# Two-pass 64-bit weight conversion with signs from GpSimd, and layer norm's Newton steps per group of tiles

## The chip, the cores and the metric

One core of a Trainium2 chip runs the whole program. The metric is device time in microseconds for one execution, with all inputs in device memory before and the output there after it.

## What is computed

Eight batches go through three blocks. The first is an attention with 32 memory slots per head; the second mixes the tokens by a low-rank product and applies a wide two-layer network (512 to 2048 to 512); the third is a gated network whose gate is layer-normalised and mixed over the tokens.

```python
a = softmax(phi, axis=seq)                 # 8 batches, 8 heads, 576 tokens, 32 slots
k_m, v_m = a.T @ k, a.T @ v
x = softmax(q @ k_m.T / 8) @ v_m           # heads joined: 8 x 576 x 512
u = x + (x.T @ U @ V).T
y = u + relu(u @ w_ch1) @ w_ch2            # 512 -> 2048 -> 512
h = relu(y @ w_in);  u, v = h[..., :512], h[..., 512:]
v_n = (v - mean(v)) / sqrt(var(v) + 1e-6)
out = (u * (w_spatial @ v_n + b_spatial)) @ w_out
```

U, V, w_ch1, w_ch2, w_in and w_out arrive as 64-bit floats (they are products of 32-bit arrays and 64-bit scalars), so the kernel turns them into 32-bit floats on the chip. The other inputs are 32-bit.

## The kernel before

Tokens stand in tiles of 128 (four, and one of 64), the 512 features in four blocks of 128. From batch 1 on, each matmul runs as three products of 16-bit high and low parts; batch 0 runs its large matmuls in 32 bits, while the weights are still being loaded, converted and split.

**Conversion.** `conv_stream` (L868) works through 22 chunks of 128 x 1024 weights: per quarter c of w_ch1 two chunks of w_ch1 and two of w_ch2, then four of w_in and two of w_out (chunks 20 and 21). A chunk is 1 MB of 64-bit words and lands in one of seven buffers, which `seq` names: two in the later z tile, two in the w_in tile, one each in those of w_out, of the spatial weights and of y (yraw). `load` (L894) lets a chunk be loaded only when the chunk that had its buffer has been converted. The loads, like all other DMAs, are issued from SP in order.

A raw chunk is read as pairs of 32-bit words, low and high. `conv_a` (L166): ScalarE (ACT) takes the absolute value of the high word into the destination, scaled so that a shift by three gives the 32-bit exponent (L167); VectorE (DVE) moves the top three bits of the low word down by 13 within 16-bit halves (L169) and keeps the sign bit of the high word beside them (L170). `conv_b` (L172): DVE shifts the destination left by three and joins it with these bits (L174). Then `square` (L911) squares the converted chunk on ACT (L182 for w_ch1, L184 for the others, in `conv_square`); for w_ch1 PE sums the squares over partitions (L918) and DVE takes their maximum (L920). After the last chunk of a weight `scale_w` (L238) finds its scale through DVE, PE (L125), DVE (L127, L144) and GpSimd (POOL; L110 and L108 are the lines of the helper `ps2`). GpSimd has no other part in the conversion.

**Order.** The program is traced in a fixed order, and a scheduler places each instruction on its engine; an engine then works strictly in that order. The `Filler` (L830) mixes the conversion into batch 0's matmuls: a call `fl(4.0, cs)` in `batch0` (L1071) advances the conversion's generator until the costs it yields (0.7 after conv_a, 1.2 after conv_b) use up the budget. `need(n)` advances it until n chunks are converted. `behind(i)` (L905) puts the DVE instructions of chunks 3 and up behind the first attention's last DVE pass (`marks[2]`, a subtraction at L404); chunks 0 to 2 may be placed among the first attention's passes. The first attention (`att(0)`, L302) also converts U and V (`setup_small`, L199) with the same two functions.

Batch 0's first half of tokens runs in four quarters c: `z_first` (L525, eviction L537), `w1_first` (L539, matmuls L547, evictions L549), then `w2_start` and `w2_add` (L565, L570). The second half follows, during which the spatial weights are loaded (L1106), the remaining weights are split (L136 to L141) and batch 1's attention runs.

**Layer norm.** `v_tile` (L677) multiplies a token tile with half of w_in (L701), evicts it through Relu (L705), takes mean and variance on DVE (L707, L709), and finds 1/sqrt(var + 1e-6) by a shift, a subtraction and three Newton steps on one column (L721 to L731), each of which is two passes of `ps2` (L110). Then the mean is subtracted (L732). The last tile's 64 tokens stand as two halves of 256 features on 128 partitions, whose statistics are joined first (L710 to L720). `v_norm` (L735) scales the tile into its 16-bit parts on ACT and DVE (L739, L745 for the last tile). `V_ORDER` (L22) fixes how v_tile (v), v_norm (n) and u_half (u, L756) follow each other: v0 first, then the string. `spatial` (L779) needs all five tiles, the last one at L795.

## Time and profile before

| | us |
|---|---|
| three runs | 1213.47, 1216.18, 1216.71 (median 1216.18) |
| the profiled execution | 1213.53 |
| its span, first to last instruction | 1211.7 |
| PE matmuls busy | 1154.9 (95%) |
| DVE busy | 751.8 (62%) |
| ACT busy | 534.4 (44%) |
| POOL busy | 66.0 (5%) |

Batch 0 takes roughly the first 260 us, each later batch 138. The engines' names in the profile are PE (TensorE), DVE (VectorE), ACT (ScalarE), POOL (GpSimd) and SP (the DMA queue). Busy shares are means over the span, in which the stages have different limits. Times in a row count from the span's start.

### The profile page before, as it was taken

What the parts mean: (1) busy time and instruction counts of PE and PEld (TensorE: products, weight loads), DVE (VectorE), ACT (ScalarE), POOL (GpSimd) and SP (SyncE); (2) the same over time, 40 slices, a digit from 0 to 9 for tenths busy, and PEclk for the clock granted to TensorE, in tenths of its full rate; (3) what the DMA queues carried; (4) which work ended last, traced back from release to release, by engine and by line L of the source; (5) the groups of instructions that cost most, each with busy time, mean ns of one, the idle gap of its engine ahead of it and who ended that gap; (6) DMA issues with size and microseconds to landing.
All of it is one profiled execution on the core that took longest, in us unless ns stands there. A gap on an engine that the chain in (4) does not pass through costs nothing.

```text
span 1211.7 us, 24362 instructions
## 1 busy us (share of the span) xinstructions
PE 1154.9 (95%) x9988; PEld 861.4 (71%) x9991; DVE 751.8 (62%) x2107; ACT 534.4 (44%) x1213; POOL 66.0 (5%) x245
## 2 busy tenths in 40 slices
PE   5767999999999999999999999999999999999998
PEld 4534676667767787677768786677767787677766
DVE  5998567856756474755657465654658455642464
ACT  2655885565534342451434433442334424342333
POOL 1003000000000000000000000000000000000000
PEclk8789999999999999999999999999999999999999
DMA  9566330014000310014000220014000210010001
GB/s 331 209 236 233 129 100 21 1 41 138 22 1 21 119 40 21 1 40 139 21 1 14 92 74 21 1 40 130 26 6 1 75 31 2 1 40 2 1 1 40
DMA packets 45680, 74.61 MB, mean 62 GB/s; under 512 B 7232, under 2 KB 36544, under 8 KB 42624
## 3 DMA queue, kind: packets, MB, share of 16 engines
q1 hardware_dynamic: 45568, 73.05, 18.4%
q8 instruction: 78, 1.28, 0.5%
q14 instruction: 34, 0.28, 0.1%
HBM read 63.60 MB, written 9.44 MB: 60 GB/s over the span
## 4 chain that ended last, share of the span: by engine, by line
PE 81%; DVE 11%; DMA 4%; ACT 2%; POOL 1%; issue 1%; SPq 0%; DVEq 0%; ACTq 0%; POOLq 0%
PE mm L630 25%; PE mm L593 14%; PE mm L816 8%; PE mm L756 7%; PE mm L793 7%; PE mm L701 6%; PE mm L570 3%; PE at L380 2%; DMA kvt<-in_kv_dram 2%; PE at L518 1%; PE at L328 1%; PE at L417 1%; PE mm L547 1%; PE mm L698 1%; DMA yraw<-in_u_dram 1%
## 5 line engine op out<-in xcount | busy, mean ns | idle before, releaser
L630 PE MATMUL mm<-g,w2r 128*128 128x288 f16 x2688 | 347.5, 286 | 0.0
L630 PEld LDWEIGHTS <-w2r 128*128 128x128 f16 x2688 | 256.9, 98 | 76.0 <-issue 14.2
L593 PE MATMUL mm<-apr,z 128*128 128x288 f16 x1344 | 167.5, 286 | 0.0
L593 PEld LDWEIGHTS <-z 128*128 128x128 f16 x1344 | 131.2, 98 | 32.9
L648 ACT ACTIVATE y<-mm 128x288 f32<-128x288 f32 x56 | 22.7, 406 | 208.7 <-DVE tiny L131 208.7
L602 DVE TENSOR_TENSOR g<-tmp,g 128x288 f16<-128x288 f32 x224 | 99.2, 456 | 20.0 <-ACT g L599 16.7
L131 DVE TENSOR_REDUCE tiny<-mm 128x1 f32<-128x288 f32 x64 | 28.8, 453 | 126.4 <-PE mm L630 124.0
L793 PE MATMUL mm<-wsr,vu 128*128 128x288 f16 x768 | 104.7, 286 | 0.0
L597 ACT ACTIVATE tmp<-mm 128x288 f32<-128x288 f32 x224 | 91.8, 422 | 28.6 <-PE mm L593 14.5
L816 PE MATMUL mm<-ghl,wor 128*128 128x288 f16 x768 | 96.9, 286 | 1.2 <-ACT wor L140 1.2
L756 PE MATMUL mm<-yhl,wir 128*128 128x288 f16 x768 | 96.8, 286 | 0.0
L816 PEld LDWEIGHTS <-wor 128*128 128x128 f16 x768 | 74.7, 98 | 22.1 <-ACT wor L140 1.5
L756 PEld LDWEIGHTS <-wir 128*128 128x128 f16 x768 | 74.5, 98 | 21.6 <-issue 1.6
L793 PEld LDWEIGHTS <-vu 128*128 128x128 f16 x768 | 74.5, 98 | 18.5
L701 PE MATMUL mm<-wir,yhl 128*128 128x512 f16 x384 | 86.0, 379 | 0.0
L803 ACT ACTIVATE ghl<-vu,ysc 128x288 f16<-128x288 f32 x64 | 34.2, 534 | 81.5 <-DVE vu L802 60.1
L701 PEld LDWEIGHTS <-yhl 128*128 128x128 f16 x384 | 37.2, 98 | 41.7 <-issue 0.3
L570 PE MATMUL mm<-g,w2r 128*128 128x288 f32 x256 | 66.6, 413 | 0.2 <-issue 0.2
L570 PEld LDWEIGHTS mm<-g,w2r 128*128 128x128 f32 x256 | 48.3, 193 | 17.1 <-issue 2.7
L110 DVE TENSOR_SCALAR tiny<-tiny 128x1 f32<-128x1 f32 x240 | 57.1, 240 | 4.1
L601 DVE CAST g<-tmp 128x288 f16<-128x288 f32 x112 | 34.4, 307 | 40.4 <-ACT tmp L597 39.8
L599 ACT ACTIVATE g<-mm 128x288 f16<-128x288 f32 x112 | 46.7, 417 | 0.0
(231 smaller groups left out, 1548.5 us busy)
## 6 DMA issues: line engine op xcount, KB each, us to landing
kvt<-in_kv_dram SPq DMA_DIRECT2D x28, 516.0 KB, 4.4
out_dram<-tmp SPq DMA_DIRECT2D x64, 144.0 KB, 1.7
qt<-in_qT_dram SPq DMA_DIRECT2D x28, 256.0 KB, 3.3
wir<-in_w_dram SPq DMA_DIRECT2D x6, 1024.0 KB, 4.8
phiT<-in_phiT_dram SPq DMA_DIRECT2D x8, 576.0 KB, 3.8
e<-in_phi_dram SPq DMA_DIRECT2D x8, 512.0 KB, 4.5
wor<-in_w_dram SPq DMA_DIRECT2D x3, 1024.0 KB, 7.0
wsr<-in_w_dram SPq DMA_DIRECT2D x3, 1024.0 KB, 4.8
```

Of the source, the lines that this page charges most:

```text
L110: eng.tensor_scalar(out=o, in0=i, scalar1=s1, scalar2=s2, op0=op0, op1=op1)
L570: pe.matmul(ps, w2r[:, f, d * 128:(d + 1) * 128], AT[0]["g"][:, f, :], start=False, stop=(f == 15))
L593: pe.matmul(ps, a["z"][:, k, x, f * 128:(f + 1) * 128], a["apr"][:, k, y, sl], start=(i == 0), stop=(i == 5))
L597: act.activation(r, ps, func=ACTF.Relu, scale=CG)
L599: act.activation(g[:, f, 0, :], ps, func=ACTF.Relu, scale=CG)
L601: dve.tensor_copy(g[:, f, 0, :], r)
L602: dve.tensor_tensor(out=g[:, f, 1, :], in0=r, in1=g[:, f, 0, :], op=ALU.subtract)
L630: pe.matmul(pss[d], w2h[:, f, x, d * 128:(d + 1) * 128], g[:, f, y, :], start=False, stop=(f == 15 and i == 2))
L701: pe.matmul(ps, yhl[:, k, x, s * 128:(s + 1) * 128], wih[:, k, 1, y, :], start=(i == 0), stop=(i == 11))
L756: pe.matmul(ps, wih[:, k, 0, x, d * 128:(d + 1) * 128], a["yhl"][:, k, y, sl], start=(i == 0), stop=(i == 11))
L793: pe.matmul(ps, vn[:, s, x, ds], wsh[:, s, th, y, :], start=(i == 0), stop=False)
L816: pe.matmul(ps, woh[:, k, x, d * 128:(d + 1) * 128], a["ghl"][:, k, y, sl], start=(i == 0), stop=(i == 11))
```

## The change

The conversion: the two 16-bit DVE passes leave `conv_a`. GpSimd instead multiplies the high words, read as 32-bit floats, by zero and by one in place, which leaves a zero with their sign. `conv_b` gets one more DVE pass, which shifts the low words right by 29 and joins them with those signs. The stream is turned by one step: conv_a of chunk i+1 is traced ahead of conv_b of chunk i. Chunk 2's DVE passes too stand behind the first attention (FREE). Chunk 21 uses the buffer of chunk 19 (yraw) instead of that of chunk 20. Chunk 0's load is issued behind the first q tiles instead of ahead of them. Of the constants only the identity is loaded, 128 x 128 instead of 128 x 512.

Layer norm: mean and variance of tiles 0 and 1, and of tiles 2 to 4, go into a common tile; the Newton steps run once per group, on two or three columns, in three passes a step instead of two. The mean is subtracted ahead of them.

```diff
@@ -19,6 +19,7 @@
 TH = S // 2
 NST = 5
 
+FREE = 2
 V_ORDER = 'v1 n0 u00 u01 v2 n1 v3 v4 n2 u02 u03 n3 n4 u10 u11 u12 u13'
 Z_ORDER = 'z0 z1 o0 z2 o1 z3 o2 o3'
 
@@ -70,8 +71,7 @@
             return tp.tile([128, n], dt, tag="tinyw", name="tinyw", bufs=4)
         return tp.tile([128, n], dt, tag="tiny", name="tiny", bufs=40)
 
-    cst = cp.tile([128, 4, 128], F32, name="cst")
-    ident = cst[:, 0, :]
+    ident = cp.tile([128, 128], F32, name="ident")
     kmt = cp.tile([128, 4, 2, M], F32, name="kmt")
     identb = cp.tile([128, 128], BF16, name="identb")
     ident16 = cp.tile([128, 128], F16, name="ident16")
@@ -151,7 +151,7 @@
             pe.matmul(ps[:, 0:256], onesb, warm_rhs, start=True, stop=True)
 
     def load_static():
-        sp.dma_start(cst, consts.rearrange("p (a c) -> p a c", a=4))
+        sp.dma_start(ident, consts[:, 0:128])
         dve.memset(onesb, 1.0)
         pool.memset(ones32, 1.0)
         pool.memset(kmt, 0.0)
@@ -164,13 +164,15 @@
         return x.rearrange("p (a c) -> p a c", a=dst.shape[1]) if len(dst.shape) == 3 else x
 
     def conv_a(dst, raw):
+
         act.activation(dst, halves(raw, dst, 1).bitcast(F32), func=ACTF.Abs, scale=2.0 ** -112)
-        q = raw.rearrange("p c w -> p (c w)").bitcast(U16).rearrange("p (c h) -> p c h", h=4)
-        dve.tensor_scalar(out=q[:, :, 0], in0=q[:, :, 1], scalar1=13, scalar2=None, op0=ALU.logical_shift_right)
-        dve.tensor_scalar(out=q[:, :, 1], in0=q[:, :, 3], scalar1=0x8000, scalar2=None, op0=ALU.bitwise_and)
+        h = raw[:, :, 1].bitcast(F32)
+        pool.tensor_scalar(out=h, in0=h, scalar1=0.0, scalar2=1.0, op0=ALU.mult, op1=ALU.mult)
 
     def conv_b(dst, raw):
         di = dst.bitcast(I32)
+        dve.scalar_tensor_tensor(out=raw[:, :, 0], in0=raw[:, :, 0], scalar=29, in1=raw[:, :, 1],
+                                 op0=ALU.logical_shift_right, op1=ALU.bitwise_or)
         dve.scalar_tensor_tensor(out=di, in0=di, scalar=3, in1=halves(raw, dst, 0), op0=ALU.logical_shift_left,
                                  op1=ALU.bitwise_or)
 
@@ -705,10 +707,15 @@
         act.activation(v, ps, func=ACTF.Relu, scale=inv)
         bs = tiny(6)
         dve.bn_stats(bs, v)
-        mv = tiny(2)
-        dve.bn_aggr(mv, bs)
-        if s == 4:
-            q, m = tiny(2), mv
+        grp, i = (0, s) if s < 2 else (1, s - 2)
+        if i == 0:
+            a["mv", grp] = tp.tile([128, 3, 2], F32, tag="mv", name="mv", bufs=2)
+        mv = a["mv", grp][:, i, :]
+        if s < 4:
+            dve.bn_aggr(mv, bs)
+        else:
+            q, m, o = tiny(2), tiny(2), mv
+            dve.bn_aggr(m, bs)
             dve.tensor_copy(q[0:64], m[64:128])
             dve.tensor_copy(q[64:128], m[0:64])
             mv, t = tiny(2), tiny(2)
@@ -717,20 +724,29 @@
             dve.tensor_scalar(out=mv, in0=m[:, 0:2], scalar1=0.5, scalar2=None, op0=ALU.mult)
             dve.scalar_tensor_tensor(out=mv, in0=q, scalar=0.5, in1=mv, op0=ALU.mult, op1=ALU.add)
             dve.tensor_tensor(out=t[:, 1:2], in0=t[:, 0:1], in1=t[:, 0:1], op=ALU.mult)
-            dve.tensor_tensor(out=mv[:, 1:2], in0=mv[:, 1:2], in1=t[:, 1:2], op=ALU.add)
-        ve = tiny(4)
-        x, y, w, hx = (ve[:, i:i + 1] for i in range(4))
-        dve.tensor_scalar(out=x, in0=mv[:, 1:2], scalar1=1e-6, scalar2=None, op0=ALU.add)
-        hv = tiny(1, I32)
+            dve.tensor_tensor(out=o[:, 1:2], in0=mv[:, 1:2], in1=t[:, 1:2], op=ALU.add)
+            dve.tensor_copy(o[:, 0:1], mv[:, 0:1])
+            mv = o
+        dve.tensor_scalar(out=v, in0=v, scalar1=mv[:, 0:1], scalar2=None, op0=ALU.subtract)
+        if s in (1, 4):
+            v_rsqrt(b, grp, i + 1)
+        return v, a["mv", grp][:, i, 1:2]
+
+    def v_rsqrt(b, grp, n):
+
+        var = AT[b]["mv", grp][:, 0:n, 1]
+        ve = tp.tile([128, 4, 3], F32, tag="ve", name="ve", bufs=2)
+        x, y, w, hx = (ve[:, i, 0:n] for i in range(4))
+        dve.tensor_scalar(out=x, in0=var, scalar1=1e-6, scalar2=None, op0=ALU.add)
+        hv = w.bitcast(I32)
         dve.tensor_single_scalar(hv, x.bitcast(I32), 1, op=ALU.logical_shift_right)
         dve.tensor_scalar(out=y.bitcast(I32), in0=hv, scalar1=-1.0, scalar2=float(0x643759DF),
                           op0=ALU.mult, op1=ALU.add)
         dve.tensor_scalar(out=hx, in0=x, scalar1=-(2.0 ** -21), scalar2=None, op0=ALU.mult)
         for it in range(3):
-            ps2(dve, w, y, y, ALU.mult, hx, ALU.mult)
-            ps2(dve, y, w, 1.5, ALU.add, y, ALU.mult)
-        dve.tensor_scalar(out=v, in0=v, scalar1=mv[:, 0:1], scalar2=None, op0=ALU.subtract)
-        return v, y
+            dve.tensor_tensor(out=w, in0=y, in1=y, op=ALU.mult)
+            dve.tensor_tensor(out=w, in0=w, in1=hx, op=ALU.mult)
+            dve.scalar_tensor_tensor(out=var if it == 2 else y, in0=w, scalar=1.5, in1=y, op0=ALU.add, op1=ALU.mult)
 
     def v_norm(b, s, v, rs):
         vn = AT[b]["vn"]
@@ -875,7 +891,7 @@
         slot = {"z0": view(rz), "z1": view(rz, 2048), "i0": view(ri), "i1": view(ri, 2048),
                 "o": view(wor.rearrange("p a c -> p (a c)")), "s": view(wsr.rearrange("p a b c -> p (a b c)")),
                 "y": view(yraw)}
-        seq = "z0 z1 i0 i1 o s y i0 i1 o s y i0 i1 o s y o s y s s".split()
+        seq = "z0 z1 i0 i1 o s y i0 i1 o s y i0 i1 o s y o s y s y".split()
         prev = [max([j for j in range(i) if seq[j] == seq[i]], default=-1) for i in range(22)]
         ch = []
         for c in range(4):
@@ -904,7 +920,7 @@
 
         def behind(i):
             st = ExitStack()
-            if i >= 3:
+            if i >= FREE:
                 st.enter_context(tc.issue_after(marks[2]))
             return st
 
@@ -920,11 +936,15 @@
                     dve.tensor_reduce(out=am[:, i // 4:i // 4 + 1], in_=sqs[0], axis=AX.X, op=ALU.max)
 
         yield
+        load(7)
+        conv_a(ch[0][1], z[0])
+        yield 0.7
         for i in range(22):
-            load(i + 7)
-            with behind(i):
-                conv_a(ch[i][1], z[i])
-            yield 0.7
+            if i < 21:
+                load(i + 8)
+                with behind(i + 1):
+                    conv_a(ch[i + 1][1], z[i + 1])
+                yield 0.7
             with behind(i):
                 conv_b(ch[i][1], z[i])
             prog[0] = i + 1
@@ -1011,7 +1031,6 @@
         vr.append((tmp()[:96, 0:TH], yi[:96, o:o + 576].rearrange("p (c w) -> p c w", w=2)))
     for (_, z), src in zip(vr, (u3, v3[:, 0:TH], v3[:, TH:])):
         conv_load(src, z)
-    ld(0)
     load_first_q()
     ld(5)
     g0 = att(0)
```

## Rows read from the trace of the kernel before

**Rows 1.** The page: span, and busy time, share and instructions of each engine.

```profile
span 1211.7 us, 24362 instructions
PE 1154.9 (95%) x9988; PEld 861.4 (71%) x9991; DVE 751.8 (62%) x2107; ACT 534.4 (44%) x1213; POOL 66.0 (5%) x245
```

**Rows 2.** Windows: length, then busy time (and instructions) by engine.

```profile
core 0: us, PE busy (x) PEld busy (x) DVE busy (x) ACT busy (x) POOL busy (x), PEclk, DMA share, GB/s
22.00:45.30 23.30, 18.93 (x114) 15.78 (x115) 22.15 (x43) 11.09 (x16) 2.97 (x8) 0.69 0.67 273
...
54.80:121.30 66.50, 46.68 (x221) 30.34 (x223) 62.43 (x75) 39.71 (x61) 9.96 (x9) 0.92 0.67 239
121.30:130.00 8.70, 8.68 (x29) 6.58 (x30) 3.87 (x3) 4.05 (x8) 0.00 (x0) 0.80 0.41 153
130.00:150.00 20.00, 17.27 (x121) 12.02 (x123) 11.84 (x31) 18.89 (x53) 2.47 (x7) 1.00 0.34 124
...
347.24:484.82 137.58, 137.09 (x1266) 103.37 (x1265) 82.06 (x248) 53.56 (x129) 6.35 (x28) 1.00 0.14 44
```

**Rows 3.** What PE waited for in the whole span: us, times, longest.

```profile
PE mm L918 <- ACT tmp L182: 10.0, 4, 5.7
...
PE at L547 <- ACT z L537: 6.2, 4, 2.4
...
PE mm L795 <- DVE vu L745: 1.4, 1, 1.4
```

**Rows 4.** Timeline of DVE, one chunk: start, us, instruction.

```profile
79.54 1.31 DVE L169 TENSOR_SCALAR wir<-wir 128x1024 uint16<-128x1024 uint16 x1
80.88 1.30 DVE L170 TENSOR_SCALAR wir<-wir 128x1024 uint16<-128x1024 uint16 x1
82.29 1.23 DVE L174 SCALAR_TENSOR_TENSOR w1r<-w1r,wir 128x1024 int32<-128x1024 int32 x1
83.43 1.30 DVE L169 TENSOR_SCALAR wir<-wir 128x1024 uint16<-128x1024 uint16 x1
```

**Rows 5.** Timeline of DVE: end of the first attention's passes; chunks 20 and 21.

```profile
44.86 0.41 DVE L404 TENSOR_TENSOR ahl<-tmp,ahl 64x256 f16<-64x256 f32 x1
...
118.37 1.23 DVE L174 SCALAR_TENSOR_TENSOR wor<-wor,wsr 128x1024 int32<-128x1024 int32 x1
124.62 1.31 DVE L169 TENSOR_SCALAR wsr<-wsr 128x1024 uint16<-128x1024 uint16 x1 [5.02 <-DMA wsr<-in_w_out_dram]
```

**Rows 6.** Timeline of PE: the last quarter's first matmuls; batch 1's last tile.

```profile
121.32 5.84 PE L547 MATMUL at<-apr,z 128*128 128x288 f32 x16 [2.39 <-ACT z L537]
...
372.25 0.29 PE L795 MATMUL mm<-wsr,vu 128*128 128x288 f16 x1
```

**Rows 7.** Timeline of POOL: memsets, and operations of one column.

```profile
0.71 0.20 POOL L156 MEMSET ones<- 128x128 f32 x1 [0.29 <-POOLq L1223]
0.86 0.31 POOL L157 MEMSET kmt<- 128x256 f32 x1
...
97.48 1.26 POOL L110 TENSOR_SCALAR st<-tiny 128x1 f32<-128x1 f32 x1 [69.76 <-DVE tiny L192]
...
103.60 2.33 POOL L108 TENSOR_SCALAR st<-st 128x1 f32<-128x1 f32 x1 [0.28 <-DVE st L144]
...
145.57 0.22 POOL L110 TENSOR_SCALAR ysc<-tiny 128x1 f32<-128x1 f32 x1 [11.62 <-DVE tiny L127]
```

**Rows 8.** Timeline of DVE, beside two of these operations.

```profile
97.39 1.32 DVE L170 TENSOR_SCALAR yraw<-yraw 128x1024 uint16<-128x1024 uint16 x1
...
103.43 1.22 DVE L174 SCALAR_TENSOR_TENSOR wir<-wir,wor 128x1024 int32<-128x1024 int32 x1
104.58 1.32 DVE L169 TENSOR_SCALAR wsr<-wsr 128x1024 uint16<-128x1024 uint16 x1
```

**Rows 9.** Timeline of DVE in batch 1's layer norm.

```profile
357.71 1.64 DVE L110 TENSOR_SCALAR tiny<-tiny 128x1 f32<-128x1 f32 x6
...
370.79 1.01 DVE L745 SCALAR_TENSOR_TENSOR vu<-tmp,tiny,vu 64x256 f16<-64x256 f32 x2 [0.57 <-ACT vu L744]
```

## The prediction, made before the changed kernel ran

> **What bounds the kernel now.** I began with the engine totals: PE is busy for 1154.9 of the 1211.7 us span [rows 1], so a change on VectorE can only pay where PE is not full. The windows say where that is [rows 2]. In a later batch (347.24 to 484.82) PE is busy 137.09 of 137.58 us. In batch 0 it is not: from 54.8, where its first large matmuls start, to 121.3 PE works 46.68 of 66.5 us, while DVE works 62.43, and in the first attention (22.0 to 45.3) DVE works 22.15 of 23.3 us. Then I asked what PE waits for [rows 3]: 10.0 us for ScalarE's squares (L182), 6.2 us for z (L537), and once, in batch 0, 1.4 us for v_norm (L745). All but the last stand behind the conversion of the 22 weight chunks in the instruction orders. The DVE timeline of one chunk [rows 4] shows two 16-bit passes (L169, L170) and one 32-bit pass (L174): from 79.54 to 83.43, 3.89 us a chunk. Chunk 20 is done at 118.37 + 1.23 = 119.60 [rows 5], and PE's last quarter of the first half of batch 0 starts at 121.32, after 2.39 us of waiting [rows 6]. So from 22 to 119.6 the end is set by DVE, and 21 chunks at 3.89 are 81.7 of these 97.6 us.
>
> **What the change does, with prices.** The profiled execution took 1213.53 us (span 1211.7); the median of the runs is 2.65 us above it, and I add that at the end.
>
> *DVE passes.* Per chunk L169 and L170 go: 80.88 - 79.54 + 82.29 - 80.88 = 2.75 us. One more pass of L174's kind comes: 1.14 (its step to the next pass, 83.43 - 82.29) to 1.34 us (1.23 and the gap of 0.11 that L174 shows behind the L170 it depends on). I take 1.34, since the second pass reads what the first writes: 1.34 + 1.14 = 2.48 instead of 3.89, 1.41 less. Over 21 chunks that is 29.6 us; DVE alone would reach the end of chunk 20 at 90.0.
>
> *Signs on GpSimd.* The trace holds no GpSimd pass of 1024 elements. Nearest are its memsets [rows 7]: 128 more elements cost 0.31 - 0.20 = 0.11 us, so 1024 elements take 0.31 + 6 x 0.11 = 0.97 us. That is the lower price. The upper one is twice that, 1.94 us, if reading and writing (a memset only writes) do not overlap. I take 1.0, near the row. The GPSIMD Engine Reference of the Trainium skill (Engine selection) calls one-input passes roughly line-rate, which at its 1.2 GHz would be an estimated 0.85 us; the memset rows agree, though no run here shows a GpSimd read of this size.
>
> *What the sign passes cost DVE.* The rows show that the engines do not run independently: a one-column GpSimd operation takes 0.22 us at 145.57 with DVE idle, but 1.26 us at 97.48, ending at 98.74, just behind the L170 that ran from 97.39 to 98.71; and the one at 103.60 took 2.33 us, to 105.93, past the end of an L174 and of the L169 behind it [rows 7, 8]. So a sign pass waits for DVE, and I must allow that DVE waits for a sign pass. From both sides: nothing, or 21 x 1.0 = 21 us. Free of charge are DVE's idle times (1.15 + 4.07 us in the two windows [rows 2]) and some of the 16 us of attention and maximum passes that read PSUM or one column: together I put 8 us as hidden and 13 as paid, since the blocked rows are nearer to paying. The rule in the Trainium skill is SBUF — State Buffer (SBUF: two separate sides): the second port pair is an exclusive lock between GpSimd and a VectorE instruction in a 2-port mode or with two SBUF inputs, and whoever is second waits for the whole instruction. The rows above agree for the one direction; by the rule all 21 us would be paid and the conversion would gain 9 instead of 17 us.
>
> *Order.* Chunk 2's DVE passes move behind the first attention's last pass (44.86 [rows 5]), and chunks 0 and 1 lose 1.41 us each, so that attention's DVE part has 3.89 + 2.8 = 6.7 us less beside it, and ends some 5 us earlier, at about 40, with 2 allowed for sign passes in the way. These microseconds are part of the 29.6, since chunk 2 comes later. Chunk 0's load goes behind q: its passes have attention's own DVE work (23.3 - 3 x 3.89 = 11.6 us) to hide behind; bounds -2 to +2, I take 0. ScalarE's Abs and the sign of chunk i+1 now stand ahead of chunk i's passes and square. This removes a wait (Abs done before DVE comes), and adds one: on ACT, chunk i's square and all z and g evictions stand behind a load that may not have landed; on GpSimd, the scale operations (L110, L108), for which DVE's reciprocal waits, stand behind a sign and its load. DVE's first pass waits for the sign, and the second pass, the maxima and the next attention's passes stand behind it.
>
> *Loads.* Chunk 20 reuses chunk 18's buffer. The end of the trace prices such a turn: DVE sat idle 5.02 us for chunk 21's load, after chunk 20 had freed its buffer [rows 5]. A turn is then 5.0 + 1.0 (the sign) + 2.48 = 8.5 us, against 2 x 2.48 + some 1.5 of other passes = 6.5: about 2 us given back. On SP nothing else is held up: chunk 21 now waits for chunk 19 instead of 20, so its 5.02 us of idle DVE mostly go, and the spatial weights' load no longer waits for chunk 21. From 121.3 to 130 ACT works 4.05 of 8.7 us and from 130 to 150 18.89 of 20, with PE at 17.27 [rows 2]: what ACT starts earlier there can give PE back up to 2.7 us; I take 1, and let ACT's new waits take it again.
>
> *PE as a floor.* If attention ends 5 us earlier, PE starts its 46.7 us of work at 50 and, with some 5 us of waits for evictions left, could not begin the last quarter before 101 to 102. That caps the gain at about 19.
>
> *Newton's steps.* Ten small passes per tile become thirteen per group of tiles. The six steps of a tile took 1.64 us [rows 9], five tiles 8.2; nine steps at no more than 0.27 each are 2.5 a group, 4.9 in all: 3.3 us less DVE work, less one copy. It is off the path: v_norm of tile 4 ended at 371.80, and PE came to it at 372.25 [rows 6, 9]. Tiles 2 and 3 must now wait for tile 4's variance, but DVE has lost the steps in between. I expect the last v_norm 0 to 1 us earlier, and count nothing; with the 0.45 us of cover gone it would cost its lateness in each of 8 batches. In batch 0 the 1.4 us wait [rows 3] may go; up to -1.
>
> The smaller constants and the three small conversions of setup: under 0.5 us either way, beside loads; 0.
>
> **Sum.** -29.6 + 13 + 2 = about -15; ACT's and GpSimd's new waits, that fall now on DVE which had none, 1: -14. The profiled time becomes 1199.5; with 2.65, 1202.
>
> **Rivals.**
> 1. *The sign passes run beside DVE.* For it: GpSimd may work ahead as far as loads have landed, seven chunks at the start; against it: rows 7 and 8. Then PE's floor and the load turns bind: -19 to -21, 1196.
> 2. *Every sign pass stops DVE.* Port time per chunk is 2.48 + 1.0 = 3.48 against 3.89: 21 x 0.41 = -9, and the load turn's 2 given back: -7, 1209. The rule of the Trainium skill named above would give this.
> 3. *Slower: the sign pass is long.* The place is DVE's first pass waiting for GpSimd; it decides from 3.89 - 2.48 = 1.41 us of unhidden sign per chunk. At 1.94 a chunk costs 4.42: 21 x 0.53 = +11, less 5 of attention's freed passes and idle time: about +6, 1222. For it: a sign pass reads and writes with a stride of two words, and lost its turn twice in succession at 103.60. Against it: 0.11 us per 128 elements.
> 4. *No change:* loads or ScalarE take DVE's place at the old pace. ACT works 39.71 of 66.5 us [rows 2], so it would need waits of 20 us: 1215.
>
> **Chances.** Forecast 0.42 (its own range 1199 to 1206); rival 1 0.20; rival 2 0.20; rival 3 0.13; rival 4 0.05. A change under 0.3% (3.6 us) cannot be told from none here. Rival 2's outcome lies close to that line, so 0.05 of it counts as no change. Faster 0.77, same 0.10, slower 0.13. The range takes in rival 1 with PE's 5 us of eviction waits gone too, rival 2, and the sign's price up to 1.4 us: 1191 to 1215.
>
> **What would show it.** Right: one-chunk steps on DVE of 2.5 to 3.3 us; GpSimd passes of 1 us when alone; chunk 20 done near 104 to 106; the wait for L182 cut by half; DVE's idle time in 54.8 to 121.3 put down to GpSimd and loads; the batches from 1 on as long as before. Wrong: DVE passes of more than 1.3 us, or steps of 3.4 and more (rival 2), sign passes of 1.5 us and more with DVE waiting for them (rival 3), chunk 20 done by 100 with PE full (rival 1), or a PE wait for L745 in every batch.

## The result, and the profile after

The changed kernel took 1203.14 us in the median of four runs (1201.71 to 1207.39), the kernel before 1215.38 beside it: a ratio of 0.9912, 95% interval 0.9895 to 0.9928. The forecast was 1202.0, in a range of 1191 to 1215. The profiled execution took 1203.14 us too, 10.4 less than the one before; so the 2.65 us that the prediction added for the difference between profile and median were not there this time. TensorE's granted clock, a mean over the span, differs from run to run and goes with the time: 0.982 in the changed kernel's longest run (1207.39), 0.990 in its shortest (1201.71). It does not explain the gain: at 0.987 the changed kernel took 1203.15, the kernel before, in seven runs beside the experiments, 1212.5 to 1214.1.

The page after, to be held against [rows 1]: 10.4 us less span, 39 us less DVE work, 27 us more on GpSimd, PE's work nearly the same.

```profile
span 1201.3 us, 24250 instructions
PE 1153.5 (96%) x9987; PEld 858.9 (71%) x9991; DVE 712.4 (59%) x1898; ACT 533.4 (44%) x1213; POOL 93.3 (8%) x270
```

Two windows that answer to those of [rows 2]: PE's large matmuls up to the last quarter of the first half, and a later batch.

```profile
48.90:106.60 57.70, 46.76 (x219) 29.21 (x222) 48.84 (x56) 40.47 (x61) 24.71 (x21) 1.00 0.75 275
...
336.22:473.80 137.58, 137.08 (x1267) 103.36 (x1265) 79.48 (x225) 53.34 (x129) 6.42 (x28) 1.00 0.14 44
```

The stretch in which PE does 46.7 us of work has become 57.7 us long, from 66.5. A later batch still takes 137.6 us from its first w_in matmul to the next batch's, although DVE does 2.6 us less in it. All of the gain lies in batch 0.

The timeline of DVE: the first attention's last pass (L406), three chunks in the middle, the pass beside a later sign, and the ends of chunks 19, 20 and 21. L174 is the first 32-bit pass, L176 the second.

```profile
40.90 0.41 DVE L406 TENSOR_TENSOR ahl<-tmp,ahl 64x256 f16<-64x256 f32 x1
...
74.99 1.23 DVE L174 SCALAR_TENSOR_TENSOR wir<-wir 128x1024 int32<-128x1024 int32 x1 [1.04 <-POOL wir L170]
76.32 2.17 DVE L176 SCALAR_TENSOR_TENSOR w1r<-w1r,wir 128x1024 int32<-128x1024 int32 x1
78.42 1.21 DVE L174 SCALAR_TENSOR_TENSOR wir<-wir 128x1024 int32<-128x1024 int32 x1
79.74 1.23 DVE L176 SCALAR_TENSOR_TENSOR w1r<-w1r,wir 128x1024 int32<-128x1024 int32 x1
82.01 1.23 DVE L174 SCALAR_TENSOR_TENSOR wor<-wor 128x1024 int32<-128x1024 int32 x1 [1.05 <-POOL wor L170]
83.15 0.68 DVE L936 TENSOR_REDUCE amw<-mm 128x1 f32<-128x512 f32 x1
83.75 1.75 DVE L176 SCALAR_TENSOR_TENSOR w2r<-w2r,wor 128x1024 int32<-128x1024 int32 x1
...
100.08 1.22 DVE L176 SCALAR_TENSOR_TENSOR wir<-wir,wsr 128x1024 int32<-128x1024 int32 x1
...
103.71 1.23 DVE L176 SCALAR_TENSOR_TENSOR wir<-wir,yraw 128x1024 int32<-128x1024 int32 x1
...
111.12 1.23 DVE L176 SCALAR_TENSOR_TENSOR wor<-wor,wsr 128x1024 int32<-128x1024 int32 x1
114.38 1.23 DVE L174 SCALAR_TENSOR_TENSOR yraw<-yraw 128x1024 int32<-128x1024 int32 x1 [2.04 <-POOL yraw L170]
115.71 1.23 DVE L176 SCALAR_TENSOR_TENSOR wor<-wor,yraw 128x1024 int32<-128x1024 int32 x1
```

The attention ends at 41.31 instead of 45.27 [rows 5]. From there to the end of chunk 19 (104.94) 18 chunks pass in 63.6 us, 3.53 a chunk, other DVE work and all waits included. Beside that work, two things make it more than the two passes: some second passes last 1.75 and 2.17 us instead of 1.23, and some first passes begin after a wait of 1 to 2 us for GpSimd. Chunk 20 is done at 112.35 (119.60 before), chunk 21 at 116.94.

GpSimd's timeline shows the sign passes (L170) in the same stretch.

```profile
43.45 1.10 POOL L170 TENSOR_SCALAR wor<-wor 128x1024 f32<-128x1024 f32 x1
...
76.32 1.11 POOL L170 TENSOR_SCALAR wir<-wir 128x1024 f32<-128x1024 f32 x1 [1.36 <-ACT w1r L168]
...
83.30 1.14 POOL L170 TENSOR_SCALAR wsr<-wsr 128x1024 f32<-128x1024 f32 x1 [1.32 <-DVE wor L174]
...
100.09 2.26 POOL L170 TENSOR_SCALAR yraw<-yraw 128x1024 f32<-128x1024 f32 x1
```

Alone a sign pass takes 1.10 to 1.16 us. Read beside DVE's rows: the sign of 83.30 ends at 84.44, and the DVE pass that was started at 83.75 ends at 85.50, 1.06 us later: it stood until the sign was through. The pass of 76.32 lasted longer by 0.94 us, most of the sign that started at the same time. The maximum at 83.15, which reads PSUM, kept its 0.68 us. The other way round, the sign of 100.09, started 0.01 us after an L176 of 1.22 us (100.08), took 2.26. So whichever comes second stands until the first is through. The Trainium skill's SBUF — State Buffer (SBUF: two separate sides) says this of a GpSimd operation that reads SBUF and a VectorE instruction with two SBUF inputs, and these rows agree. The second thing shows in the brackets of both timelines: the sign overwrites the high words that ScalarE's absolute value (L168) reads, and so stands behind it, and DVE's first pass behind the sign. Over 20 to 130 us DVE's waits for the signs add up:

```profile
DVE yraw L174 <- POOL yraw L170: 4.4, 3, 2.0
DVE wsr L174 <- POOL wsr L170: 3.6, 3, 1.5
...
DVE wor L174 <- POOL wor L170: 1.0, 1, 1.0
DVE wir L174 <- POOL wir L170: 1.0, 1, 1.0
```

Then the end of the stream. Before, chunk 21's last pass, the load of the spatial weights behind it on SP, and ScalarE's first splitting pass of w_in (three views of the kernel before: DVE, SP, ACT):

```profile
127.73 1.23 DVE L174 SCALAR_TENSOR_TENSOR wor<-wor,wsr 128x1024 int32<-128x1024 int32 x1 [0.42 <-ACT wor L167]
```

```profile
128.98 0.33 SPq L1106 DMA_DIRECT2D wsr<-in_w_sp_dram  x1
```

```profile
130.04 1.32 ACT L136 ACTIVATE tmp<-wir,st 128x512 f32<-128x512 f32 x2
```

And the same two of the changed kernel (SP, ACT). Its chunk 21 ended at 116.94, and the splitting still stands behind it; the load doesn't any more: the buffer of the spatial weights is now free with chunk 20, and the load is issued 0.06 us behind that chunk's end (112.35).

```profile
112.41 0.33 SPq L1125 DMA_DIRECT2D wsr<-in_w_sp_dram  x1
```

```profile
118.03 1.32 ACT L136 ACTIVATE tmp<-wir,st 128x512 f32<-128x512 f32 x2
```

All three moved 12 to 17 us. On PE (its timeline after) the last quarter starts at 106.65 instead of 121.32 [rows 6], 14.7 us earlier, but then PE waits 3.27 us for a kv tile. By batch 1's first large matmul the lead is 11.0 us.

```profile
106.65 0.75 PE L549 MATMUL at<-apr,z 128*128 128x288 f32 x2 [2.60 <-ACT z L539]
...
129.58 1.09 PE L330 MATMUL at<-kvt,e 128*32 128x129 f32 x16 [3.27 <-DMA kvt<-in_kv_dram]
```

### The profile page after: what moved, and what is told of

Same layout as the page of the kernel before. It is cut to its first block, busy times and chain, and to the rows that moved or that the text cites. A ratio compares the mean times of both kernels' runs of the same rounds, so it can differ in the third digit from the quotient of the medians.

```text
span 1201.3 us, 24250 instructions
## 1 busy us (share of the span) xinstructions
PE 1153.5 (96%) x9987; PEld 858.9 (71%) x9991; DVE 712.4 (59%) x1898; ACT 533.4 (44%) x1213; POOL 93.3 (8%) x270
## 4 chain that ended last, share of the span: by engine, by line
PE 84%; DVE 6%; DMA 3%; POOL 2%; ACT 2%; issue 2%; SPq 0%; POOLq 0%; DVEq 0%; ACTq 0%
PE mm L632 25%; PE mm L595 14%; PE mm L772 8%; PE mm L809 8%; PE mm L832 8%; PE mm L703 7%; PE at L382 3%; DMA kvt<-in_kv_dram 3%; PE mm L572 2%; PE at L330 2%; PE at L520 1%; PE at L419 1%; PE mm L700 1%; PE mm L625 1%; PE at L457 1%
## 5 line engine op out<-in xcount | busy, mean ns | idle before, releaser
L604 DVE TENSOR_TENSOR g<-tmp,g 128x288 f16<-128x288 f32 x224 | 99.3, 456 | 20.0 <-ACT g L601 16.6
L110 POOL TENSOR_SCALAR ysc<-tiny 128x1 f32<-128x1 f32 x32 | 8.7, 271 | 571.7 <-DVE tiny L127 394.3
L836 ACT ACTIVATE tmp<-mm,ysc 128x288 f32<-128x288 f32 x64 | 31.5, 496 | 35.9 <-PE mm L832 34.9
```

Source lines behind the costliest of these rows:

```text
L604: dve.tensor_tensor(out=g[:, f, 1, :], in0=r, in1=g[:, f, 0, :], op=ALU.subtract)
```

## The experiments

Times are medians; the kernel before ran beside each group on the same chip (1214.9, 1214.3, 1213.8 and 1213.5 us in the four groups). Theory P: the sign passes block DVE (rival 2 of the prediction). Theory L: the chain of load, absolute value and sign is late.

**1. no_sign.** No sign pass at all (the signs and the lowest mantissa bits are left out).

```diff
-        pool.tensor_scalar(out=h, in0=h, scalar1=0.0, scalar2=1.0, op0=ALU.mult, op1=ALU.mult)
...
-                                 op0=ALU.logical_shift_right, op1=ALU.bitwise_or)
+                                 op0=ALU.logical_shift_right, op1=ALU.bitwise_and)
```

> The changed kernel without GpSimd's sign passes; the first DVE pass has the same operands and takes an 'and' in place of the 'or'. The signs and the last mantissa bits of the converted weights are left out. Theory P (port): in the changed kernel DVE passes that run beside a sign pass are longer by 9.6 us in all (1.6 to 2.2 us instead of 1.22), and DVE waits about 11 us more for signs, so nearly all of the 21 x 1.1 us is paid. Without them every L174 and L176 pass is back at 1.2 us, the step per chunk falls from 3.5 to 2.5 to 2.8, chunk 20 is done at 95 to 102 instead of 112.35, and PE's 46.8 us of work becomes the floor: 1195 to 1199 us. Theory L (loads and ScalarE's pass hold the stream): the passes get shorter, but DVE waits for ScalarE or for loads instead; chunk 20 not before 108; total within 3 us of 1203.

Measured 1196.09 (ratio 0.9834, 0.981 to 0.9858). Every pass is back at 1.21 to 1.25, and chunk 20 is done at 101.87 + 1.22 = 103.09, 9.3 us earlier than with the signs:

```profile
101.87 1.22 DVE L174 SCALAR_TENSOR_TENSOR wor<-wor,wsr 128x1024 int32<-128x1024 int32 x1
```

The sign passes cost the changed kernel 7 us by the medians, 9 by the ratios. The mean step per chunk, measured as above from the first attention's end to the end of chunk 19, is (99.11 - 43.96) / 18 = 3.06.

**2. sign_unread.** As 1, but GpSimd reads the same words and writes 16-bit zeros into a scratch that nobody reads, so that nothing waits for the result. (The edit also gives the pool of small tiles 28 buffers instead of 40.)

```diff
+        sg = tp.tile([128, 1024], BF16, tag="sg", name="sg", bufs=1)[:raw.shape[0], 0:n]
+        pool.tensor_scalar(out=sg, in0=raw[:, :, 1].bitcast(F32), scalar1=0.0, scalar2=1.0, op0=ALU.mult, op1=ALU.mult)
```

> As no_sign (signs and last mantissa bits left out), but GpSimd runs a pass of the same 1024 strided elements per chunk, into a 16-bit scratch tile that nobody reads. Theory P splits into its two parts here: the passes that were lengthened stay long, 7 to 10 us in all, but the waits of DVE for a sign are gone: chunk 20 at 101 to 107, 1198 to 1201 us. If the cost were the wait alone (sign behind ScalarE's pass, DVE behind the sign) and not the port, this run equals no_sign within 1.5 us. If it were the port alone, it equals the changed kernel within 1.5 us.

Measured 1204.8 (0.9916, 0.9896 to 0.9935), the changed kernel's time but for 1.7 us by the medians and 0.5 by the ratios. No DVE pass waits for a sign here, yet passes are long again; one of them on DVE and the GpSimd pass beside it:

```profile
74.68 2.19 DVE L175 SCALAR_TENSOR_TENSOR yraw<-yraw 128x1024 int32<-128x1024 int32 x1
```

```profile
74.65 1.14 POOL L171 TENSOR_SCALAR sg<-wir 128x1024 bf16<-128x1024 f32 x1 [1.57 <-DMA wir<-in_w_dram]
```

The pass is longer by 0.97 us, the length of GpSimd's pass less little. GpSimd's passes give the whole loss even where nothing waits for them; the lateness of the signs adds nothing that the time shows. P stands, L falls.

**3. sign_dve.** The same multiplication on DVE, in conv_b ahead of the first pass, instead of in conv_a on GpSimd.

```diff
-        pool.tensor_scalar(out=h, in0=h, scalar1=0.0, scalar2=1.0, op0=ALU.mult, op1=ALU.mult)
+        dve.tensor_scalar(out=h, in0=h, scalar1=0.0, scalar2=1.0, op0=ALU.mult, op1=ALU.mult)
```

> The sign pass of the changed kernel moved from GpSimd to DVE, right ahead of the two passes: three DVE passes a chunk as before the change, but of 32 bits. Theory P: nothing of a sign is hidden on GpSimd, so what counts is what the pass costs on DVE. At 1.3 us, as the 16-bit passes took (1.30 to 1.35): step 3.8, chunk 20 at 116 to 119, 1205 to 1209 us. At half rate's cost, 0.7 us, as the contiguous 128x512 pass (0.48 us) suggests: step 3.2, chunk 20 at 105 to 108, 1198 to 1202 us. Theory L: DVE's extra pass is beside the waits; within 2 us of 1203 at either price.

Measured 1202.33 (0.9898, 0.9875 to 0.992). The DVE timeline of one chunk, from first pass to first pass 2.87 us; the sign (L173) takes 0.70:

```profile
79.80 1.23 DVE L174 SCALAR_TENSOR_TENSOR wir<-wir 128x1024 int32<-128x1024 int32 x1
80.94 0.70 DVE L173 TENSOR_SCALAR wir<-wir 128x1024 f32<-128x1024 f32 x1
81.54 1.23 DVE L176 SCALAR_TENSOR_TENSOR w1r<-w1r,wir 128x1024 int32<-128x1024 int32 x1
82.67 1.23 DVE L174 SCALAR_TENSOR_TENSOR wir<-wir 128x1024 int32<-128x1024 int32 x1
```

GpSimd's help is worth nothing in the changed kernel: DVE does the same sign in 0.70 us, for which GpSimd stops it for some 1.0. This chunk is an undisturbed one: the mean step, other work and waits included, was 3.49, and chunk 20 ended at 113.97 where the expectation had 105 to 108. The time fits theory L's expectation as well, so this run alone does not choose between P and L.

**4. sign_act.** A ScalarE pass in GpSimd's place (a copy scaled by zero, in place; the signs are left out).

```diff
-        pool.tensor_scalar(out=h, in0=h, scalar1=0.0, scalar2=1.0, op0=ALU.mult, op1=ALU.mult)
+        act.activation(h, h, func=ACTF.Copy, scale=0.0)
```

> The sign pass moved from GpSimd to ScalarE, right behind its absolute value (a copy scaled by zero, in place). Theory P: DVE passes are all 1.2 us again; ScalarE gets 22 x 1.1 = 24 us more beside its 40.5 of 57.7 us in the stretch from 48.9 to 106.6, and becomes the bound: 1202 to 1208 us, with DVE's waits put down to ScalarE. Theory L: the chain from load over absolute value and sign to DVE is as long as before and the squares stand behind it: 1205 to 1212 us, DVE passes 1.2 us too. A time under 1201 would say that the port is worth more than ScalarE's 24 us.

Measured 1207.03 (0.9934, 0.9913 to 0.9954). DVE's passes are short, but now DVE waits 10.1 us for ScalarE in wsr's chunks alone, and PE 10.5 for the squares. Of the three engines ScalarE is the worst place.

**5 to 7. The change in three parts.** conv_only is the kernel before with the hunks of conv_a and conv_b alone (the diff below), newton_only the kernel before with the hunks of v_tile and v_rsqrt alone; order_only is the changed kernel with the diff below turned round, so it has the new order, buffers, loads and Newton steps with the old conversion.

```diff
-        dve.tensor_scalar(out=q[:, :, 0], in0=q[:, :, 1], scalar1=13, scalar2=None, op0=ALU.logical_shift_right)
-        dve.tensor_scalar(out=q[:, :, 1], in0=q[:, :, 3], scalar1=0x8000, scalar2=None, op0=ALU.bitwise_and)
+        pool.tensor_scalar(out=h, in0=h, scalar1=0.0, scalar2=1.0, op0=ALU.mult, op1=ALU.mult)
...
+        dve.scalar_tensor_tensor(out=raw[:, :, 0], in0=raw[:, :, 0], scalar=29, in1=raw[:, :, 1],
+                                 op0=ALU.logical_shift_right, op1=ALU.bitwise_or)
```

> The kernel before with the new conversion alone (two 32-bit passes, sign on GpSimd); the stream's order, the buffers, the first loads and Newton's steps as before. Theory P (a sign pass of 1.1 us stops VectorE's two-input passes for most of its length, so a chunk costs 2.5 + 1.1 = 3.6 instead of 3.9 us): 21 x 0.3 = 6 us less work on VectorE, chunk 20 done at 112 to 115, PE's last quarter still behind chunk 20's square; time 1208 to 1212. Theory L (the wait load, absolute value, sign is the loss, because the stream looks too little ahead): without the turned stream it gets worse, VectorE waits for GpSimd at each chunk; 1214 to 1218. If the order added nothing at all, it equals the changed kernel, 1203.

> The changed kernel with the old 16-bit passes in place of the sign pass and the second 32-bit pass; turned stream, chunk 2 behind the first attention, buffers, loads and grouped Newton steps as changed. Theory P with order (PE's last quarter no longer stands behind chunk 20's square but behind chunk 19's, worth some 6 us, on top of the conversion's 6): steps of 4.0 us a chunk, first attention's last pass 3 to 5 us earlier, chunk 20 done at 117 to 121, yet the last quarter starts at 111 to 117 instead of 121; time 1206 to 1211. Without an order effect: 1213 to 1217.

> The kernel before with the grouped Newton steps alone. As the prediction has it (off the path in the later batches, up to 1 us in batch 0's wait for the last v_norm): 1213 to 1216, every later batch within 0.3 us of before. If the steps had been on the path in each batch: 8 x 0.5 = 4 less, 1211; if waiting for tile 4 delays tiles 2 and 3: 1218 and more, with a PE wait for v_norm in each batch.

Measured: conv_only 1212.01 (0.9984, 0.9972 to 0.9996), order_only 1210.55 (0.9972, 0.9958 to 0.9986), newton_only 1214.97 (1.0009, 1.0 to 1.0019). The Newton steps are worth nothing, as predicted. But the parts gain 2.3 and 3.8 us, 6 together, where the change gains some 11 to 12. Both times lie within or at the edge of what I had expected, but order_only not for its reason: its chunk 20 ended at 121.99 and PE's last quarter started at 124.53, both later than in the kernel before. Why the two parts don't add up shows in DVE's timeline of conv_only:

```profile
122.46 1.23 DVE L174 SCALAR_TENSOR_TENSOR wsr<-wsr 128x1024 int32<-128x1024 int32 x1 [7.36 <-POOL wsr L170]
123.79 1.23 DVE L176 SCALAR_TENSOR_TENSOR wor<-wor,wsr 128x1024 int32<-128x1024 int32 x1
```

Chunk 20 ended at 115.11, 4.5 us earlier than before, but chunk 21 shares its buffer, and DVE stood 7.36 us for the load, the absolute value and the sign. In order_only the buffer is another, but DVE is as slow as before: chunk 21 ends at 127.54. Only both together bring chunk 21 forward. So a new theory, T: what counts is the end of chunk 21, behind which the splitting of w_in and w_out stands (and, where chunk 21 has the spatial weights' buffer, their load), not that of chunk 20 and PE's last quarter (theory C, the prediction's).

**8. kv_later.** Two more yields per token tile in batch 1's attention, to move its kv products apart.

```diff
+                if b == 1:
+                    yield
+                    yield
```

> The changed kernel with two more yields per token tile in batch 1's attention (its k and v products spread wider among batch 0's second half, so the later ones meet their loads later). Theory G (of the 14.7 us by which PE's last quarter started earlier, 3 to 4 us are given back at the wait for the kv tile's load of 3.3 us and in the lower clock behind it): the wait goes or falls under 1 us; time 1199 to 1201. If the lost microseconds are set elsewhere (the weights' split, dgb, the end of batch 1's attention): 1202 to 1205, a later wait takes its place.

Measured 1206.22 (0.9934, 0.9919 to 0.9948), slower than the changed kernel by 3 and outside both expectations. The edit missed its place: the third tile's products still came right behind the first two's, with a wait of 2.87 us, and only the later parts of that attention moved back. Nor can the 3 us be laid on the edit by this profile: chunk 21 ended 2.4 us later than in the changed kernel, 1.5 of them already at the end of the first attention (42.78), which the edit leaves alone. Whether that wait costs anything stays open.

**9 and 10. One buffer, both ways.** after_s is the changed kernel with chunk 21 in chunk 20's buffer again (the diff; chunk 21's conv_a then has to follow chunk 20's conv_b); conv_y is conv_only with the first two lines turned round.

```diff
-        seq = "z0 z1 i0 i1 o s y i0 i1 o s y i0 i1 o s y o s y s y".split()
+        seq = "z0 z1 i0 i1 o s y i0 i1 o s y i0 i1 o s y o s y s s".split()
...
-            if i < 21:
+            if i < 20:
...
+            if i == 20:
+                with behind(21):
+                    conv_a(ch[21][1], z[21])
```

> The changed kernel with one thing put back: chunk 21 is loaded into the buffer of chunk 20 again, not of chunk 19 (and so its absolute value and sign follow chunk 20's passes). Theory T (what the change gained is the end of chunk 21, behind which the spatial weights' load and the splitting of w_in and w_out stand; chunk 21 ended at 116.9 in the changed kernel, 129.0 before, 125.0 with the conversion alone, 127.5 with the order alone): a load turn of 5.0 + 1.15 + 1.1 + 2.45 = 9.7 us stands between chunk 20 (112.4) and the end of chunk 21, which comes at 121 to 123; time 1206 to 1209. Theory C (the end of chunk 20 and PE's last quarter set it, as the prediction had it): 1202 to 1204.

> The conversion alone (1212.0) with one thing added: chunk 21 is loaded into the buffer of chunk 19. Theory T: chunk 21's load starts some 6 to 8 us earlier, its end comes at 117 to 120 instead of 125.0; time 1204 to 1208. Theory C: chunk 20 still ends at 115, so 1211 to 1213. If the turned stream (absolute value and sign a step ahead) were the part that the conversion alone lacked: 1210 to 1213 too, with VectorE waiting for GpSimd at each chunk, and chunk 20's end unchanged.

Measured: after_s 1208.68 (0.9957, 0.9945 to 0.9969), 5.5 us more than the changed kernel; conv_y 1207.50 (0.9955, 0.9942 to 0.9968), 3.5 by the ratios to 4.5 by the medians less than conv_only. The DVE rows of chunk 21, of after_s and of conv_y:

```profile
121.23 1.23 DVE L174 SCALAR_TENSOR_TENSOR wsr<-wsr 128x1024 int32<-128x1024 int32 x1 [7.33 <-POOL wsr L170]
122.37 1.21 DVE L317 TENSOR_TENSOR e<-e,at 128x1024 f32<-128x1024 f32 x1
123.50 1.22 DVE L176 SCALAR_TENSOR_TENSOR wor<-wor,wsr 128x1024 int32<-128x1024 int32 x1
```

```profile
119.16 1.23 DVE L176 SCALAR_TENSOR_TENSOR wor<-wor,yraw 128x1024 int32<-128x1024 int32 x1
```

Against theory C speak the starts of PE's last quarter, in PE's timelines of after_s, of conv_only and of conv_y: with after_s it starts 1.5 us later than in the changed kernel, but the time is 5.5 longer; conv_y starts it 1.8 us later than conv_only and is faster.

```profile
108.17 0.75 PE L549 MATMUL at<-apr,z 128*128 128x288 f32 x2 [2.61 <-ACT z L539]
```

```profile
114.97 1.24 PE L549 MATMUL at<-apr,z 128*128 128x288 f32 x4 [0.74 <-ACT z L539]
```

```profile
116.73 0.51 PE L549 MATMUL at<-apr,z 128*128 128x288 f32 x1 [0.76 <-ACT z L539]
```

And sign_unread starts it at 114.89, 8.2 us later than the changed kernel, at nearly the same time. T stands for both. The change of one letter in a string, with what follows from it, is 3.5 to 5.5 us of the whole gain.

PE's waits in after_s show the way from chunk 21 to PE:

```profile
PE at L330 <- ACT e L320: 4.1, 1, 4.1
...
PE mm L832 <- ACT wor L140: 2.1, 1, 2.1
```

In the changed kernel the first is 0.4 and the second is missing. L317, in the DVE rows above, is a pass of batch 1's attention. DVE works in order, so it had to stand with chunk 21's first pass until 122.37; ScalarE's exponential (L320) and PE's kv products (L330) wait for it. L140 is the splitting. So in this pair it is the DVE order and the splitting, and no wait for the spatial weights is among PE's larger ones. In the pair of conv_only and conv_y the difference is spread over several waits of at most 1.4 us.

**11. sign_mix.** With P and T together: signs on GpSimd only for U, V and chunks 0 to 2, whose passes stand among the first attention's; from chunk 3 on DVE takes them (a third argument, late, leaves the GpSimd pass out of conv_a and puts the DVE pass of experiment 3 into conv_b).

```diff
-                    conv_a(ch[i + 1][1], z[i + 1])
+                    conv_a(ch[i + 1][1], z[i + 1], i > 1)
...
-                conv_b(ch[i][1], z[i])
+                conv_b(ch[i][1], z[i], i > 2)
```

> The changed kernel with the signs of chunks 0 to 2 and of U and V still on GpSimd, but those of chunks 3 to 21 on VectorE (0.69 us each, no GpSimd pass beside the two-input passes). The first attention ends as in the changed kernel (41.3, against 44.6 with all signs on VectorE), and the steps behind it take 3.0 to 3.2 us instead of 3.53: 18 x 0.4 = 7 us, less the loads' waits. By theory P and T chunk 21 ends at 111 to 114 and the time is 1198 to 1201. If PE's own work or the loads take VectorE's place from there: 1201 to 1204, the same as with the signs wholly on one engine.

Measured 1194.63 (1193.52 to 1197.75; ratio 0.9844, 0.9829 to 0.9859): 19 us less than before, 8 less than the changed kernel, and faster than expected. It beats both. One chunk in DVE's timeline, sign (L176) to sign 2.87 us, and chunk 21's last pass:

```profile
79.26 0.69 DVE L176 TENSOR_SCALAR wor<-wor 128x1024 f32<-128x1024 f32 x1
...
82.13 0.69 DVE L176 TENSOR_SCALAR wsr<-wsr 128x1024 f32<-128x1024 f32 x1
...
111.18 1.22 DVE L179 SCALAR_TENSOR_TENSOR wor<-wor,yraw 128x1024 int32<-128x1024 int32 x1
```

One step of the expectation failed: the first attention ended at 43.86, not 41.3. The mean step was 3.24.

**12. sign_small.** As 11, with the signs of chunks 0 to 2 on DVE as well.

```diff
-        conv_a(ch[0][1], z[0])
+        conv_a(ch[0][1], z[0], True)
...
-                    conv_a(ch[i + 1][1], z[i + 1], i > 1)
+                    conv_a(ch[i + 1][1], z[i + 1], True)
...
-                conv_b(ch[i][1], z[i], i > 2)
+                conv_b(ch[i][1], z[i], True)
```

> All 22 chunks' signs on VectorE, only those of U and V (two small passes early in the first attention) on GpSimd: between the kernel with all signs on VectorE (1202.3) and that with chunks 0 to 2 on GpSimd as well (1194.6). If GpSimd's three passes inside the first attention are what that one gains: VectorE has 3 x 0.69 = 2.1 us more before the attention's last pass, time 1196 to 1198. If U and V's signs are the whole of it: 1194 to 1195. If the 7.7 us come from the stall of 3.3 us at 58 to 63 (VectorE behind ScalarE and PE) and the lower clock in the kernel with all signs on VectorE, which has nothing to do with those three passes: either near 1194 or near 1202, depending on whether that stall is there.

Measured 1197.03 (0.9861, 0.9838 to 0.9885). The number falls into the first expectation, its reason doesn't: the attention ended earlier (39.38) than in sign_mix, not later. What separates these two from sign_dve (1202.3), which does nearly the same work, is not settled. In sign_dve DVE waits 2.0 us for ScalarE and 1.3 for PE between 58 and 63; sign_small has only one such wait, 1.29 for PE. Part of it goes with the granted clock: 0.983 to 0.989 in sign_dve's runs, 0.985 to 0.993 in sign_small's. At 0.989 sign_dve took 1200.47, and at 0.990 sign_small 1196.87 to 1199.31.

**The end of chunk 21 beside the time.** From each profiled execution, differences to the one before (128.96 and 1213.53, at a granted clock of 0.984), and its granted clock:

| kernel | end of chunk 21 | time | clock |
|---|---|---|---|
| newton_only | +0.8 | +3.7 | 0.979 |
| order_only | -1.4 | -3.0 | 0.984 |
| conv_only | -3.9 | -3.7 | 0.987 |
| after_s | -4.2 | -5.9 | 0.987 |
| conv_y | -8.6 | -7.5 | 0.984 |
| kv_later | -9.7 | -7.0 | 0.986 |
| sign_dve | -11.4 | -10.9 | 0.983 |
| the change | -12.0 | -10.4 | 0.990 |
| sign_unread | -12.5 | -10.1 | 0.984 |
| sign_act | -13.1 | -5.8 | 0.981 |
| sign_small | -14.1 | -14.2 | 0.990 |
| sign_mix | -16.6 | -20.0 | 0.991 |
| no_sign | -20.6 | -10.8 | 0.983 |

Three stand apart, and their clocks are among the lowest. newton_only's was 0.979. In sign_act ScalarE, which does the splitting, also has a pass more per chunk. no_sign's profiled execution was the longest of its five runs (1202.71 at 0.983, where the shortest took 1193.67 at 0.990); by its median it is at -19. And small differences in one profile are no effects: after_s has the changed kernel's stream up to chunk 20, yet its chunk 19 ended 1.5 us later. With chunk 21 that early the time stops at some 1194 to 1196 in both sign_mix and no_sign.

## Why the prediction was right

The total came out within 1.1 us, and that was luck in part: one step failed, one was missing, and the two lay on opposite sides. The added 2.65 us hid a part of it: against the profiled execution's 1199.5 the profile came out 3.6 us longer. Of the signs named for being right, the wait for the squares fell by half (10.0 to 5.0 us); but chunk 20 was not done at 104 to 106, and the mean step of 3.53 is one of the signs named for being wrong.

*DVE passes.* Right: an undisturbed pair takes 79.74 + 1.23 - 78.42 = 2.55 us, predicted 2.48.

*The sign's price.* Right in size: 1.10 to 1.16 us for the 1.0 taken from the memsets [rows 7]. The prediction's upper bound of 1.94 and with it rival 3 were out.

*What the signs cost DVE, and its waits.* Here the step failed. The prediction had chunk 20's end some 14 us earlier; it came 7.25 earlier. Three windows, from 22 to chunk 20's end, of the kernel before, of the changed kernel and of no_sign:

```profile
22.00:119.60 97.60, 71.30 (x377) 48.90 (x379) 94.01 (x125) 55.63 (x83) 12.87 (x17) 0.84 0.67 244
```

```profile
22.00:112.35 90.35, 70.26 (x368) 45.68 (x371) 77.49 (x107) 60.04 (x90) 40.02 (x39) 0.92 0.73 274
```

```profile
22.00:103.09 81.09, 68.48 (x355) 46.94 (x355) 68.11 (x104) 56.64 (x84) 7.45 (x15) 0.84 0.75 284
```

DVE's work without signs falls by 25.9 us, predicted 29.6. The sign passes lengthen it by 9.4, predicted 13. But DVE's idle time grows from 3.6 to 12.9 us, where the sum had 1 for new waits and 2 for the load turn. So the mis-sized term is the waits: in the changed kernel 7.9 us of them are waits for the sign itself, as at 74.99 and 82.01. They are no price of the signs alone, since no_sign is idle for 13.0 us too, behind ScalarE's absolute value, PE and loads instead. "8 us as hidden and 13 as paid" was thus not the right account: on DVE's rows 9.4 us of lengthened passes and 7.9 us of waits, 17 of some 23 us, belong to signs, and taking the signs away gave 9.3. Rival 2's mechanism, that a sign pass stops DVE, is shown by experiments 1 and 2; its sum of 3.48 us a chunk has no waits and no other work in it, so the measured 3.53 is near it by chance. The rows for the blocking were there: [rows 7, 8] showed one-column operations of GpSimd standing behind DVE's passes, and no row on which both ran at once.

*Order and buffer.* This was missing from the sum. I named chunk 21's 5.02 us of idle DVE [rows 5] and counted, net, nothing for it, because I held chunk 20 and PE's last quarter for the end of the path. Experiments 9 and 10 put 3.5 to 5.5 us on that buffer. The rows to look at were those behind it: the spatial weights' load at 128.98, 0.02 us behind chunk 21's last pass, and the splitting at 130.04. So rival 2's mechanism came with the forecast's time: its 1209 is what after_s measured (1208.7), the changed kernel without the other buffer.

*The turn of chunk 20's buffer.* Priced at 2 us: from chunk 19's end to chunk 20's 7.4 us passed, between the 6.5 without and the 8.5 with the turn; about right in size.

*Attention.* 4.0 us earlier, predicted some 5.

*PE's start of the last quarter.* It came to 106.65 with chunk 20 done only at 112.35: in the turned stream PE's instructions of that quarter stand behind chunk 19's square and no longer behind chunk 20's. I had not seen that. It gave less than the 14.7 us it shows, and order_only has no gain there at all.

*Newton's steps.* Right: newton_only is within 0.1% of before. In the later batches the last v_norm now ends 1.1 us ahead of PE's need (359.31 + 0.99 against 361.40; before 0.45 us ahead [rows 6, 9]). DVE's and PE's timelines of the changed kernel:

```profile
359.31 0.99 DVE L761 SCALAR_TENSOR_TENSOR vu<-tmp,mv,vu 64x256 f16<-64x256 f32 x2
```

```profile
361.40 0.29 PE L811 MATMUL mm<-wsr,vu 128*128 128x288 f16 x1
```

*PE as a floor.* Consistent as a cap: the best kernel found gains 19 to 20 us, where the prediction put the cap at about 19. That PE's work is what stopped it there is not shown.

What stays open: which of the things behind chunk 21 binds in each kernel (only after_s was followed to PE's waits); whether the wait for the kv tile costs anything; and why sign_dve is slower than sign_small. A sign pass with a buffer of its own, which would take away its wait for the absolute value, was not tried; experiment 2 says that it would gain little.

## What to carry to other kernels

Work given from VectorE to GpSimd was no help beside two-input passes: where the two meet, one stands until the other is through, so ask whether VectorE would do that work in less. When an engine gets less to do, price the waits that its other work had covered: here its idle time grew by 9 us. In a stream through shared buffers look for the last item's load turn and for what is queued behind that item: here one buffer's name was worth 3.5 to 5.5 us, the conversion alone 2.3, and the new order with that buffer but the old conversion 3.8, of some 12 together. When a sum comes out right, take the change apart all the same: here an overrated and an overlooked term had cancelled.

## What the runs showed that I had not expected

A strided 32-bit multiplication of 1024 elements took 0.69 us on DVE, a strided 16-bit shift of as many 1.31 [rows 4]: the operation that was given to GpSimd is on DVE the cheapest of the three. And small DVE operations are stopped as well: beside a sign pass (87.89, 1.42 us) the 128 x 128 scaling of L119 took 0.82 us instead of 0.25 (DVE's timeline).

```profile
88.54 0.82 DVE L119 TENSOR_SCALAR dgb<-identb,tiny 128x128 bf16<-128x128 bf16 x1
```
